# Two spectral layers and two feed-forward layers: row loads in quarters, shorter runs of zero products, statistics and residual sums placed elsewhere, the last inverse step's copies divided differently

## The chip, the cores and the metric

The kernel runs on one core of one Trainium2 chip. The metric is device time in microseconds (us) of one execution. Five executions of the kernel before the change were timed: 927.07, 926.19, 929.46, 926.41 and 926.54 us, so the median is 926.54 us. One of them (927.07 us) was recorded by the hardware profiler, and every duration below that is not a median comes from this record. Engines are written as the profile writes them: PE is TensorE, PEld its weight load, DVE is VectorE, ACT is ScalarE, POOL is GpSimd, SP is SyncE, which here only issues DMAs. A small q behind an engine's name means its sequencer.

## The reference

`x` has 2048 tokens (rows) of 1024 features in bf16. Four residual layers follow one another: A, B, A, B, the two A layers with the same weights and the two B layers with the same weights.

```python
def _A_ref(x, w_r, w_i):                      # 2D real FFT, a filter, and back
    X = rfft2(x) * (w_r + 1j * w_i)
    return irfft2(X, s=(2048, 1024))

def _B_ref(x, w1, b1, w2):                    # 1024 -> 3584 -> 1024
    h = x @ w1 + b1
    return (h * tanh(softplus(h))) @ w2       # the Mish activation

x = x + _A_ref(_layernorm(x)); x = x + _B_ref(_layernorm(x), ...)
x = x + _A_ref(_layernorm(x)); x = x + _B_ref(_layernorm(x), ...)
```

The layer norm takes mean and variance of every token over its 1024 features.

## The kernel before

**Program and waits.** The Python code writes out five instruction lists, one for each engine, in a fixed order. `op` and `group` record what an instruction reads and writes as resources (`Res`), and from them follow the semaphores that it waits for. An engine runs its list strictly in the order written, so an instruction that waits holds up everything behind it on its engine. A PSUM bank is a resource too: a copy out of a bank is noted as a writer of that bank, so a second copy from the same bank on another engine waits for the first.

**Residual stream.** `XS` holds x in SBUF as 16 tiles of 128 tokens. Statistics of a tile come either from DVE (`stats_half`, `stats_quarter`: bn_stats and bn_aggr, lines 466 to 486) or from ACT (`stats_act`, line 446): one pass with Copy and one with Square over 1024 features, each followed by a read of its accumulator. `sums_to_mv` and `scales` on DVE make mean and reciprocal root of these, and `apply` (line 522) makes the normalised tile.

**Start.** In layer 0 (the first A) SP first issues the loads of x into `XS`, then loads x a second time in another arrangement, `XR` (lines 399 to 407, issued at line 251): partition = (block of 128 tokens, feature block), 128 rows of 128 features each. This comes as one half and two quarters of the rows, each in 8 DMAs with 256-byte pieces. `r_xr` says which part a block of step s1 waits for. Behind them on SP follow the table FD, which step s2 reads, the table JT, the filters and more tables. Meanwhile DVE and ACT take the statistics of all 16 tiles.

**Layer A.** s1 (lines 619 to 647) multiplies the 16 blocks of 8 rows by the first transform matrices; in layer 0 each block has its own matrices, scaled by `scaled` with the norm (lines 604 to 617, on DVE, POOL and, for block 1, ACT). Copies out of PSUM (lines 640, 642) are on ACT and DVE. Then the list of `order_A` (line 1006) interleaves steps s2, s3, i1, i2 for 8 groups g: a word such as 310 means step 3, group 1, part 0; 4 is i1, 5 is i2. s3 ends with four DVE products (lines 800 to 807) whose result YK is what i1 (line 842) reads. PSUM is handed out as a ring of four pairs of banks in this order. i2's result goes out to HBM and comes back transposed (`u_turn`, `u_last`) as UT, in four parts for the last step i4 (line 1071).

**End of layer A.** While UT comes back, PE does `spin` (4 products), `residual_first` (8 products that put the old x into PSUM, line 1060) and `hold` (line 656): 16 products in layer 0 and 11 in layer 1 with a matrix of zeros, 128x512, which change nothing and only keep PE at work. Then, in `layer_B` from line 1507, i4 is done for tiles 0 to 3 in four parts u of 32 columns; `out_first` (line 1076) copies tiles t and t+1 of part u, 512 elements per partition, to `XS`, and `stats_quarter` takes the statistics of the part. After part 3, `root` and `apply` give the first two normalised tiles, PE transposes them (line 1181) and the first matrix product of layer B can start.

**Layer B.** `mm1` (line 1220) multiplies w1 by normalised tokens, into three PSUM banks in turn; ACT applies Mish (line 1224). `rest` mixes in the rest of i4 for tiles 4 to 15, whose result lies in `YS` until `residual` (line 1498, DVE) adds it to `XS`. The rest of w1's product is done in `quads` (lines 1250 to 1320) as a Strassen-like scheme of seven products for each of 14 blocks n (line 1260), with DVE additions (line 1265) and Mish on ACT (line 1270); `after(n)` puts statistics, `normal` and `residual` of later tiles between them. The product with w2 (line 1359) has the same kind of scheme.

Of the kernel before, what the change touches and what calls it, by code (L numbers as in the profile page):

```python
# [5 lines left out]
ACT = mybir.ActivationFunctionType  # L6
ALU = mybir.AluOpType
P = 128
# [172 lines left out]
class KB:  # L181
# [200 lines left out]
    def prologue(self):  # L382
        sp = self.sp
        self.op(self.pool, lambda e: e.memset(self.EPS[:], 1e-5), writes=[self.r_eps, self.r_warm])
        xt = self.x[0].rearrange("(t p) d -> p t d", p=P)

        for a, b in ((10, 11), (0, 1), (1, 2), (11, 12), (2, 3), (3, 4), (12, 13), (4, 6), (13, 14), (6, 8), (14, 15), (8, 10), (15, 16)):
            self.dma(self.act if a == 10 else sp, self.XS[:, a:b, :], xt[:, a:b, :], f"x{a}", writes=self.r_xs[a:b])
        self.warm(ACT.Sqrt)
        small = {}  # L390
        def load_small(name, n, d):
            b = self.alloc(name, self.o[name], [n], d)
            self.dma(sp, b.ap, self.con[name], name.lower(), writes=[b.res])
            small[name] = b
        load_small("M0", P, BF)
        load_small("IDF", P, F32)
        self.M0, self.IDF = small["M0"], small["IDF"]

        self.XR = self.alloc("XR", self.o["XR"], [P, P])
        self.r_xr = []  # L400
        xv = self.x[0].rearrange("(n2 n1) (h l) -> h n2 n1 l", n2=16, l=P)
        for q, n in ((0, 2), (2, 1), (3, 1)):
            r = Res(f"xr{q}")
            for h in range(8):
                s = slice(32 * q, 32 * (q + n))
                self.dma(sp, self.XR.ap[h:P:8, s, :], xv[h][:, s, :], f"xr{q}", parts=[r])
            self.r_xr += [r] * n
        self.dma(sp, self.FD[:], self.con["FD"], "fd", writes=[self.r_fd])
        load_small("JT", 4 * P, BF)
        self.JT, self.r_jt = small["JT"].ap, small["JT"].res  # L410
        self.w1_next = 0
# [31 lines left out]
                writes=rr)  # L443
        self.op(self.dve, lambda e: e.reciprocal(r, a), writes=rr)

    def stats_act(self, j):
        act = self.act
        x, sums, rs, junk = self.XS[:, j, :], self.BN[:, j, 0:2], self.r_mv[j], self.junk
        rs.begin()
        for i, f in enumerate((ACT.Copy, ACT.Square)):  # L450
            self.op(act, lambda e, i=i, f=f: e.activation(junk.ap, x, f, accum_out=sums[:, i:i + 1]),  # L451
                    reads=[self.r_xs[j]], writes=[junk.res], parts=[rs])

# [257 lines left out]
    def layer_A(self, li):  # L711
# [7 lines left out]
        dve, act, sp, pool = self.dve, self.act, self.sp, self.pool  # L719
# [275 lines left out]
                u_turn(g, h)  # L995
        self.spin(4, 0)
        self.residual_first()
        self.hold(11 if li else 16, 7)
        if li == 0:
            self.op(self.pool, lambda e: e.tensor_copy(self.B1[:], self.B1h[:]), reads=[self.r_b1h], writes=[self.r_b1])  # L1000
        self.w1_buf = [self.alloc(f"W1_{i}", (self.ob["WS"] + i * 4096, 140 * K)[i > 4], [8, 256]) for i in range(4 if li else 6)]
# [3 lines left out]
    @staticmethod  # L1005
    def order_A():


        order = ("200 201 210 211 300 301 220 310 400 221 311 401 230 320 410 500 231 321 411 501 330 331 420 510 240 511 421 241 "
                 "250 251 340 341 520 350 430 260 521 431 440 261 351 441 530 531 360 361 270 450 451 271 540 541 550 551 460 370 "  # L1010
                 "461 371 560 561 470 471 570 571")
        return [tuple(map(int, w)) for w in order.split()]
# [60 lines left out]
                                               stop=lo > 0 or l % k == k - 1))  # L1073
        self.group(fns, reads=self.r_ut[u0 // 32:(u0 + n - 1) // 32 + 1] + [self.r_mt], writes=self.r_bank[bank:bank - (-n // k)])

    def out_first(self, u, t, prog):

        b = slice(2 * u, 2 * u + 2)
        src = self.PS[:, b, :].rearrange("p b (i c) -> p c b i", c=32)[:, 8 * t:8 * t + 16]
        dst = self.XS[:, t:t + 2, :].rearrange("p n (h l) -> p (n h) l", l=P)[:, :, 32 * u:32 * u + 32]  # L1080

        self.copy(prog, dst.rearrange("p c (b i) -> p c b i", i=16), src, [], self.r_bank[b], parts=self.r_xs[t:t + 2])

    def i4_out(self, lo, nb, u0, n, bank, staged, r_staged, prog):

# [71 lines left out]
    def layer_B(self, li, last):  # L1157
        pe, dve, act, sp, pool = self.pe, self.dve, self.act, self.sp, self.pool
# [47 lines left out]
        def mm1(c, fg, half=None, mid=()):  # L1206
            wb = self.w1_buf[fg]
            x = XT[c]
            tok = slice(0, 512) if half is None else slice(256 * half, 256 * half + 256)
            w = tok.stop - tok.start  # L1210
            for fl in range(2):
                if fl:
                    for f in mid:
                        f()
                ft = 2 * fg + fl
                bank = nh[0] % 3
                nh[0] += 1
                fns = []
                for db in range(8):
                    fns.append(lambda e, db=db, bank=bank, fl=fl: e.matmul(  # L1220
                        PS[:, bank, 0:w], wb.ap[:, db, fl * P:(fl + 1) * P], x.ap[:, db, tok], start=(db == 0), stop=(db == 7)))
                self.group(fns, reads=[wb.res] + (r_xt[c] if half is None else [r_xt[c][half]]), writes=[self.r_bank[bank]])
                at, ra = at_of(c, ft), r_at[c % 2][ft]
                self.op(act, lambda e, bank=bank, ft=ft, at=at: e.activation(at[:, tok], PS[:, bank, 0:w], ACT.Mish,  # L1224
                                                                      bias=self.B1[:, ft:ft + 1]),
                        reads=[self.r_bank[bank], self.r_b1], writes=[ra])
# [246 lines left out]
        def at_tiles(c):  # L1473
            r_at[c] = [None] * NF
            for k in range(2):
                off = self.ob["A"] + 14336 * (2 * k + c)
                AT[c][k] = b = self.alloc(f"AT{c}{k}", off, [NF // 2, 512])
                for i in range(NF // 2):
                    r = r_at[c][2 * i + k] = Res(f"AT{c}_{2 * i + k}")
                    r.inherit(b.res)  # L1480
                    self.live.append((off + i * 1024, off + i * 1024 + 1024, r))
# [8 lines left out]
        def staged_rest(bank, n):  # L1490

            u0 = self.u0
            self.u0 += n
            self.i4(4, 12, u0, n, bank)
            return lambda: self.i4_out(4, 12, u0, n, bank, YS, r_ys, act)
# [5 lines left out]
        def turns(c, *ts):  # L1501
            return [lambda t=t: transposed(c, t, xn[4 * c + t]) for t in ts]
# [4 lines left out]
        for u in range(4):  # L1507
            self.i4(0, 4, 32 * u, 32, 2 * u)
            if u == 0:
                self.hold(2, 7)  # L1510
            self.out_first(u, 0, act)
            for j in range(2):
                self.stats_quarter(j, u)
            if u == 0:
                self.out_first(0, 2, dve)
        rests = [staged_rest(0, 10)]
        for u in range(1, 3):
            self.out_first(u, 2, act)
# [34 lines left out]
            xn[j] = self.apply(j)  # L1553
        for fg in range(1, 4):
            mm1(0, fg, 1)
            if fg < 3:
                self.stats_act(5 + fg)
        if not last:
            mm1(0, 4)
        at_tiles(1)  # L1560
        B = {"B11": (XT[0].ap[:, 0:4, :], r_xt[0]), "B21": (XT[0].ap[:, 4:8, :], r_xt[0])}
        order = list(early)
        if last:
            block, corner, run = quads(list(range(4, 14)), order, B, [k * 1024 for k in (102, 140)])
            for n, bank in ((0, 3), (1, 4), (2, 5), (3, 0)):
                block(n, bank)
            corner(1, 4)
            turns(1, 0)[0]()
            corner(2, 5)
            turns(1, 1)[0]()  # L1570
            corner(3, 0)
        else:
            mm1(0, 5, mid=turns(1, 0, 1))
# [50 lines left out]
        def after(n):  # L1624
            again = {0: 7, 4: 8, 5: 9} if last else {0: 7}
            if n in again:
                self.fill_slot(order[again[n]], plain + again[n])
            if 1 <= n < 4:
                load_b(STD, n // 3, (n - 1) % 2)
            first = 6 if last else 4  # L1630
            if last:
                if n in (0, 2, 4, 5):
                    self.stats_act(8 + (0, 2, 4, 5).index(n))
                if n == 5:
                    self.xn_buf = self.xn_out + [self.alloc(f"XN{i}", self.ob["XN2"] + i * 2048, [self.D]) for i in range(2)]
                if n in (5, 7):
                    self.sums_to_mv(n + 3, 2)
                    self.scales(n + 3, 2)
            elif n < 4:
                self.stats_dve(8 + n)  # L1640
            elif n == 4:
                self.scales(8, 4)
            if n >= first:
                normal(8 + n - first)
                turn(4)
            for j in {first + 1: (12, 13), first + 2: (14,), first + 3: (15,)}.get(n, ()):
                residual(j)
        run(after, lead)
        self.junk = self.alloc("JUNK2", self.ob["JUNK2"], [self.D])
# [68 lines left out]
        order = [ws[n % 3] for n in range(14)]  # L1718
# [94 lines left out]
```

## Time and profile before

| | |
|---|---|
| median of five executions | 926.54 us (926.19 to 929.46) |
| the profiled execution: its time, its span | 927.07 us, 925.2 us |
| busy in the span: PE, DVE, ACT, POOL | 876.8, 623.4, 434.9, 147.7 us |
| granted TensorE clock | 1.000 |
| layer 0 A; layer 0 B; layer 1 A; layer 1 B (from the timeline, rounded) | 0 to 111; 111 to 474; 474 to 560; 560 to 925 us |

The span runs from the first to the last recorded instruction; 1.87 us of the execution lie around it. A row of the timeline or of the chain has the start in us from the span's start, the duration in us, the engine and the line of the kernel; `x8` means that eight instructions were merged; what stands in brackets is the idle time of the engine before the row and what ended it. A row of the waits reads: engine and line, what ended its wait, us in total, times, the longest in us. The end of a matmul is modelled, so the start-to-start distance of two matmuls is a better measure than the shown idle time: 8 products of 128x256 follow one another every 0.87 us, 4 of 128x512 every 0.86 us.

### The profile page before, as it was taken

What the parts mean: (1) busy time and instruction counts of PE and PEld (TensorE: products, weight loads), DVE (VectorE), ACT (ScalarE), POOL (GpSimd) and SP (SyncE); (2) the same over time, 40 slices, a digit from 0 to 9 for tenths busy, and PEclk for the clock granted to TensorE, in tenths of its full rate; (3) what the DMA queues carried; (4) which work ended last, traced back from release to release, by engine and by line L of the source; (5) the groups of instructions that cost most, each with busy time, mean ns of one, the idle gap of its engine ahead of it and who ended that gap; (6) DMA issues with size and microseconds to landing.
All of it is one profiled execution on the core that took longest, in us unless ns stands there. A gap on an engine that the chain in (4) does not pass through costs nothing.

```text
span 925.2 us, 13610 instructions
## 1 busy us (share of the span) xinstructions
PE 876.8 (95%) x5503; PEld 470.2 (51%) x5503; DVE 623.4 (67%) x995; ACT 434.9 (47%) x645; POOL 147.7 (16%) x170
## 2 busy tenths in 40 slices
PE   0899899999999999999999998999999999999998
PEld 0677576444444444444446766754444444444443
DVE  7798468686889667568767765666747655554463
ACT  7898485456203475510018966757550025552000
POOL 0732004950004642010121200000000000000000
PEclk9999999999999999999999999999999999999999
DMA  9979962675796388274733786345156635732532
GB/s 279 279 254 289 224 186 72 213 256 133 265 287 232 143 322 293 107 248 140 269 92 115 224 213 161 137 167 183 32 196 187 207 139 182 274 120 85 176 125 103
DMA packets 153502, 175.98 MB, mean 190 GB/s; under 512 B 75000, under 2 KB 132568, under 8 KB 153320
## 3 DMA queue, kind: packets, MB, share of 16 engines
q1 hardware_dynamic: 140256, 130.32, 45.8%
q0 software_dynamic: 10032, 42.90, 12.6%
q10 hardware_dynamic: 3152, 1.90, 0.8%
q8 instruction: 43, 0.70, 0.3%
q14 instruction: 19, 0.16, 0.0%
HBM read 130.78 MB, written 40.89 MB: 186 GB/s over the span
## 4 chain that ended last, share of the span: by engine, by line
PE 86%; DVE 6%; ACT 4%; SPq 2%; DMA 2%; issue 1%; ACTq 0%; DVEq 0%
PE PS L1359 37%; PE PS L1260 30%; PE PS L1220 6%; PE PS L741 3%; PE PS L842 2%; SPq L251 2%; PE PS L872 2%; PE PS L1071 2%; ACT ARENA L640 1%; PE PS L1181 1%; ACT ARENA L451 1%; PE PS L904 1%; DVE ARENA L1186 1%; DMA ARENA<-in_A_x_dram 1%; ACT ARENA L573 1%
## 5 line engine op out<-in xcount | busy, mean ns | idle before, releaser
L1359 PE MATMUL PS<-ARENA 128*128 128x512 bf16 x1568 | 340.3, 379 | 0.1
L1260 PE MATMUL PS<-ARENA 128*128 128x512 bf16 (+1 forms) x1288 | 280.3, 379 | 0.8 <-DVE ARENA L1265 0.8
L1359 PEld LDWEIGHTS PS<-ARENA 128*128 128x128 bf16 x1568 | 153.2, 98 | 184.9 <-DVE ARENA L1402 0.5
L1265 DVE TENSOR_TENSOR ARENA<-PS,ARENA 128x512 f32<-128x512 f32 x230 | 157.0, 690 | 100.2 <-PE PS L1260 92.5
L1260 PEld LDWEIGHTS PS<-ARENA 128*128 128x128 bf16 x1288 | 125.4, 98 | 153.2 <-DVE ARENA L1265 3.5
L1270 ACT ACTIVATE ARENA<-ARENA,B 128x512 bf16<-128x512 f32 x138 | 98.8, 721 | 69.1 <-DVE ARENA L1265 63.8
L573 ACT ACTIVATE ARENA<-PS 128x512 f32<-128x512 f32 (+3 forms) x86 | 61.6, 726 | 110.6 <-PE PS L1260 92.5
L1153 POOL TENSOR_TENSOR ARENA<-ARENA 128x512 bf16<-128x512 bf16 x56 | 71.0, 1269 | 75.1 <-DVE ARENA L522 60.9
L451 ACT ACTIVATE ARENA<-XS 128x1024 bf16<-128x1024 bf16 x60 | 63.2, 1053 | 36.7 <-DVE XS L1410 33.2
L1220 PE MATMUL PS<-ARENA 128*128 128x256 bf16 (+1 forms) x528 | 73.4, 295 | 3.4 <-DVE ARENA L1186 1.9
L1384 DVE TENSOR_TENSOR ARENA<-ARENA 128x3584 bf16<-128x3584 bf16 x32 | 63.9, 2016 | 0.0
L1220 PEld LDWEIGHTS PS<-ARENA 128*128 128x128 bf16 x528 | 50.3, 98 | 22.3 <-DVE ARENA L1186 3.3
L1410 DVE TENSOR_TENSOR XS<-PS,ARENA 128x512 bf16<-128x512 f32 x52 | 35.7, 689 | 38.4 <-PE PS L1359 38.1
L1402 DVE TENSOR_TENSOR ARENA<-PS,ARENA 128x512 f32<-128x512 f32 x48 | 32.9, 687 | 27.4 <-PE PS L1359 27.0
L1224 ACT ACTIVATE ARENA<-PS,B 128x256 bf16<-128x256 f32 (+1 forms) x66 | 33.0, 514 | 29.0 <-PE PS L1220 28.8
L1270 ACT ACTIVATE ARENA<-PS,B 128x512 bf16<-128x512 f32 x46 | 31.5, 685 | 18.4 <-PE PS L1260 18.4
L1398 DVE TENSOR_TENSOR ARENA<-ARENA,XS 128x512 f32<-128x512 f32 x52 | 37.0, 735 | 0.6
L442 ACT ACTIVATE RS<-MV,EPS 128x1 f32<-128x1 f32 (+2 forms) x11 | 3.3, 296 | 71.5 <-DVE MV L564 70.1
L842 PE MATMUL PS<-ARENA 128*128 128x256 bf16 x256 | 32.6, 273 | 1.3 <-DVE ARENA L807 1.0
L741 PE MATMUL PS<-FD,ARENA 128*128 128x256 bf16 (+1 forms) x256 | 31.4, 271 | 2.5 <-ACT ARENA L640 2.5
L798 ACT ACTIVATE ARENA<-PS 128x1024 bf16<-128x1024 f32 x30 | 30.4, 1046 | 5.0 <-PE PS L789 5.0
L1235 DVE TENSOR_TENSOR ARENA<-ARENA 128x2048 f16<-128x2048 bf16 x16 | 25.3, 1582 | 9.0 <-PE PS L1220 8.7
(102 smaller groups left out, 810.1 us busy)
## 6 DMA issues: line engine op xcount, KB each, us to landing
ARENA<-in_B_w_dram SPq DMA_DIRECT2D x30, 896.0 KB, 6.6
ARENA<-w1s_scratch SPq DMA_DIRECT2D x28, 896.0 KB, 4.7
ARENA<-w2s_scratch SPq DMA_DIRECT2D x24, 896.0 KB, 6.3
w1s_scratch<-ARENA POOLq DMA_DIRECT2D x14, 896.0 KB, 4.3
ARENA<-in_B_w_dram SPq DMA_DIRECT2D x24, 512.0 KB, 4.5
u_scratch<-ARENA SPq DMA_DIRECT2D x14, 512.0 KB, 4.7
ARENA<-u_scratch SPq DMA_DIRECT2D x14, 512.0 KB, 5.9
w2s_scratch<-ARENA POOLq DMA_DIRECT2D x8, 896.0 KB, 4.1
```

The lines of the kernel that those rows point to most:

```text
L451: self.op(act, lambda e, i=i, f=f: e.activation(junk.ap, x, f, accum_out=sums[:, i:i + 1]), reads=[self.r_xs[j]], writes=[junk.res], parts ...
L573: fn = (lambda e: e.activation(dst, src, ACT.Copy)) if scale is None else \
L741: fns.append(lambda e: e.matmul(dst, at(r), FD[:, t:t + n], start=start, stop=stop))
L842: fns.append(lambda e, c=c, part=part: e.matmul(ps[:, c * 256:(c + 1) * 256], yk.ap[:, part, c * P:(c + 1) * P], t[:, (128, 0)[part]:(384, ...
L1153: self.op(self.pool, lambda e, dst=A(dst), x=A(x), y=A(y), op=op: e.tensor_tensor(dst, x, y, op), reads=[b.res] + list(after), writes=[b.rs])
L1220: fns.append(lambda e, db=db, bank=bank, fl=fl: e.matmul(PS[:, bank, 0:w], wb.ap[:, db, fl * P:(fl + 1) * P], x.ap[:, db, tok], start=(db ...
L1260: self.group([lambda e, db=db: e.matmul(PS[:, bank, :], A[:, db, :], mov[:, db, :], start=(start and db == 0), stop=(db == 3), skip_group_ ...
L1265: self.op(dve, lambda e: e.tensor_tensor(dst.ap, PS[:, bank, :], x.ap, ALU.add), reads=[self.r_bank[bank], x.res], writes=[dst.res])
L1270: self.op(act, lambda e: e.activation(at, src, ACT.Mish, bias=self.B1[:, ft:ft + 1]), reads=[res, self.r_b1], writes=[ra])
L1359: self.group([lambda e, i=i, k=k, b=PB[n][k].ap: e.matmul(PS[:, bank, :], ap[:, i, t * P:(t + 1) * P], b[:, i - 7 * k, :], start=(start an ...
L1384: self.op(dve, lambda e: e.tensor_tensor(ap[dst][:, f, :], ap[x][:, f, :], ap[y][:, f, :], op), reads=part(x, k) + part(y, k), writes=part ...
L1398: self.op(dve, lambda e: e.tensor_tensor(a[t], a[t], x, ALU.add), reads=[rx], writes=[r[t]])
```

## The change

Six places change.

1. `XR` is loaded in four quarters of the rows, 8 DMAs and a resource of its own each: 32 DMAs in place of 24, of the same bytes in the same 256-byte pieces.
2. `hold` does 12 zero products in place of 16 in layer 0, and 5 in place of 11 in layer 1.
3. In `order_A`, 221 (s2 of group 2, part 1) stands ahead of 400 (i1 of group 0, part 0) and no longer behind it. This holds for both A layers.
4. `out_first` takes a number of tiles. In part 3, ACT copies tile 0 and DVE tile 1 (256 elements each) where ACT copied both; in part 0, tiles 2 and 3 are copied by ACT and no longer by DVE. This holds for both B layers.
5. `stats_act` can do one of its two passes. The four passes for tiles 6 and 7 stood in pairs behind two of the `mm1` calls; now one pass stands behind each of three, and the fourth behind `mm1(0, 4)` (layer 0) or behind the first `corner` (layer 1).
6. In the last layer, `residual` of tiles 12 and 13 stands at n = 1 and n = 3 of `quads`, where both stood at n = 7. Tiles 14 and 15 stay at n = 8 and 9, and the first B layer keeps its places.

```diff
-        for q, n in ((0, 2), (2, 1), (3, 1)):
+        for q in range(4):
             r = Res(f"xr{q}")
             for h in range(8):
-                s = slice(32 * q, 32 * (q + n))
+                s = slice(32 * q, 32 * q + 32)
                 self.dma(sp, self.XR.ap[h:P:8, s, :], xv[h][:, s, :], f"xr{q}", parts=[r])
-            self.r_xr += [r] * n
+            self.r_xr.append(r)
...
-    def stats_act(self, j):
+    def stats_act(self, j, passes=(0, 1)):
...
-        rs.begin()
-        for i, f in enumerate((ACT.Copy, ACT.Square)):
+        if passes[0] == 0:
+            rs.begin()
+        for i in passes:
+            f = (ACT.Copy, ACT.Square)[i]
...
-        self.hold(11 if li else 16, 7)
+        self.hold(5 if li else 12, 7)
...
-        order = ("200 201 210 211 300 301 220 310 400 221 311 401 ...
+        order = ("200 201 210 211 300 301 220 310 221 400 311 401 ...
...
-    def out_first(self, u, t, prog):
+    def out_first(self, u, t, prog, n=2):
...
-            self.out_first(u, 0, act)
+            if u < 3:
+                self.out_first(u, 0, act)
+            else:
+                self.out_first(u, 0, act, 1)
+                self.out_first(u, 1, dve, 1)
             for j in range(2):
                 self.stats_quarter(j, u)
             if u == 0:
-                self.out_first(0, 2, dve)
+                self.out_first(0, 2, act)
...
         for fg in range(1, 4):
             mm1(0, fg, 1)
-            if fg < 3:
-                self.stats_act(5 + fg)
+            self.stats_act(6 + fg // 3, ((fg - 1) % 2,))
         if not last:
             mm1(0, 4)
+            self.stats_act(7, (1,))
...
             corner(1, 4)
+            self.stats_act(7, (1,))
             turns(1, 0)[0]()
...
-            for j in {first + 1: (12, 13), first + 2: (14,), first + 3: (15,)}.get(n, ()):
+            late = {1: (12,), 3: (13,), 8: (14,), 9: (15,)} if last else {5: (12, 13), 6: (14,), 7: (15,)}
+            for j in late.get(n, ()):
                 residual(j)
```

## The prediction

> **What bounds the kernel now.** I read the page first, then the waits of PE stage by stage, then the chain in order of time, then the timeline around each edit.
>
> ```profile
> span 925.2 us, 13610 instructions
> ...
> PE 876.8 (95%) x5503; PEld 470.2 (51%) x5503; DVE 623.4 (67%) x995; ACT 434.9 (47%) x645; POOL 147.7 (16%) x170
> ...
> PE 86%; DVE 6%; ACT 4%; SPq 2%; DMA 2%; issue 1%; ACTq 0%; DVEq 0%
> ```
>
> PE is busy for 95% and carries 86% of the chain, and no edit but the zero products takes work from it. So the change is worth what it takes out of PE's waits. The waits of PE in three windows (116 to 474, 482 to 566, 566 to the end) show which of them the edits touch:
>
> ```profile
> PE PS L1220 <- ACT ARENA L1224: 0.8, 2, 0.6
> ```
> ```profile
> PE PS L1071 <- DMA ARENA<-u_scratch: 0.9, 1, 0.9
> ...
> PE PS L842 <- DVE ARENA L807: 0.6, 1, 0.6
> ```
> ```profile
> PE PS L1260 <- DVE ARENA L1265: 0.8, 1, 0.8
> PE PS L1220 <- ACT ARENA L1224: 0.6, 1, 0.6
> ```
>
> The other PE waits in the two B layers (0.9, 0.9 and 0.4 us) belong to the transposes, and none is for a DMA. What is gained at these places should therefore arrive at the end: behind them the DMAs are released by PE's own progress and move with it.
>
> **Rows in quarters.** In the timeline SP's queue reads, in two windows (last part of the half, then quarters):
>
> ```profile
> 14.25 6.04 SPq L251 DMA_DIRECT2D ARENA<-in_A_x_dram  x5
> ```
> ```profile
> 20.34 11.27 SPq L251 DMA_DIRECT2D ARENA<-in_A_x_dram  x16
> ```
>
> A half costs 6.04/5 = 1.21 us of SP, a quarter 0.63 us and 0.67 us apart (the first, 1.20 us, still queues behind the halves). Before 14.25 the queue is held up by the loads of x, and three of the 8 half DMAs are out. In quarters that is 6, and 26 x 0.67 = 17.4 us more end at 31.7; FD is issued at 31.65 now. So nothing behind the rows (FD, JT, filters, tables, all on SP) moves by more than some 0.3 us. The first quarter lands near 19 us in place of 24.33, so s1 no longer waits 3.2 us for it, but for its matrices: DVE's first product ends at 22.73, and ACT is in block 1's matrices until 24.08. ACT's first copy goes from 25.45 to 24.1. This lead is lost by the end of s1: block 12 needs the last quarter, landed at 33.81, and starts at 33.85 now; s2 starts at 38.01, FD has landed at 37.65, and the first filter, read right after s2's first group (39.54), at 39.34. I take 0, from 0.1 less to 0.5 more.
>
> **Zero products.** The chain in order of time, layer 0 and layer 1:
>
> ```profile
> 107.36 3.45 PE PS L656 x16
> 110.82 0.79 PE PS L1071 x32
> ...
> 555.22 4.87 DMA ARENA<-u_scratch
> 560.23 0.95 PE PS L1071 x32
> ```
>
> In layer 0, UT's first part lands at 110.22, and i4 begins at 110.65 because 16 x 0.216 us of zeros end only then. Twelve end at 109.75. In layer 1 i4 starts 0.14 us after the landing (560.09), so here 110.36: 0.29 less, and part 1 (landed 111.16, needed at 111.6) doesn't take it back. In layer 1 PE waits for the landing either way: six zeros less lengthen its idle time from 1.1 to 2.4 us and gain nothing, 0. What this idle time costs is not in the trace: after 1.3 us idle (at 491.93) PE goes on at full pace; after 3.2 us (24.38) the first 8 products of s1 took 1.05 us, later ones 0.62. At the worst ratio, 1.7, on the 3.8 us of i4 and its two zeros, that is 2.5 us. I take 0, as the same 32 products took 0.95 us after 1.1 us idle and 0.95 after none; 2.5 stays as the upper end.
>
> [...]
>
> **The order of s2 and i1.** In layer 1 PE finishes s3(1,0) at 498.66 and waits for the DVE product until 499.47 (0.80 us start to start), while the s2 that stands behind i1 has its inputs. With s2(2,1) first, PE runs 498.67 to 499.54, i1 follows at once (YK is there at 499.41), and s3(1,1) starts 0.82 us earlier. ACT, busy back to back from 500.55 on, starts at 499.9 with s2's copy. DVE's products are back to back until 505.53 and stay there, but its next gap (0.66 us at 506.19, waiting for ACT) closes. The next i1 has to wait for its YK (501.41). Neither step issues a DMA. I take 0.65 less, from 0.8 to 0. In layer 0 the same swap gains nothing: DVE and ACT run without a gap from 43 to 57 us there, and PE waits for DVE at 58.36 in any case.
>
> **Copies.** Window 114.6 to 117 of the timeline, part 3 of i4 in layer 0:
>
> ```profile
> 114.31 1.23 DVE L482 BATCH_NORM_STATS2 BN<-XS 128x6 f32<-128x256 bf16 x3
> ...
> 114.48 1.57 ACT L573 ACTIVATE XS<-PS 128x512 bf16<-128x512 f32 x3 [0.20 <-PE PS L1071]
> ...
> 115.57 0.26 DVE L484 BATCH_NORM_AGGREGATE MV<-BN 128x2 f32<-128x24 f32 x1
> ```
>
> Everything after this hangs on DVE: two statistics, two aggregates, root, apply, then PE (117.58). ACT's copy of both tiles ends at 115.08, and DVE, which ends part 2's statistics at about 115.0, starts the next at 115.11. So ACT was hardly late. Now ACT's half copy ends at 114.88 (0.60 less 256 elements at 0.85 ns), DVE's copy waits for it as the bank's earlier writer, stands ahead of the statistics in DVE's queue and takes 0.41 us (0.67 for 512 elements, less 256 at 1.07 ns; overlapped with the next, 0.34). The statistics start at 115.35: 0.24 later, in both layers, 0.5 more (0.2 to 0.9). Part 0's copy on ACT fits its gap (112.24 to 112.88), and takes 0.67 us from DVE where DVE waits for ACT anyway: 0.
>
> [...]
>
> **Statistics of tiles 6 and 7.** The chain says what PE waited for at 139.27 and 142.21:
>
> ```profile
> 137.70 1.15 ACT ARENA L451 x2
> 139.58 1.05 ACT ARENA L451 x2
> 140.65 1.15 ACT ARENA L451 x2
> 142.21 3.63 PE PS L1220 x16
> ```
>
> Four passes of 1.17 us come in pairs between Mish operations, and PE, with three banks, needs the Mish of three products ago. Its product due at 138.49 (137.62 + 0.87) started at 139.27: 0.78 lost; the one due at 141.89 started at 142.21: 0.32. In layer 1 one such loss, 588.84 in place of 588.06: 0.78. With one pass for each pair of Mish (0.83 us): first pass 136.52 to 137.68, Mish of the third product 137.70 to 138.16, ahead of 138.49; the later Mish end at 138.5, 140.1, 140.5 and are needed at 139.4, 141.1, 142.8. ACT does 2.0 us for PE's 1.74 in this stretch, so it falls back 0.26 a step, for three steps, and the banks carry that. Square of tile 7 ends at 144.75 (595.2 in layer 1); DVE asks for it at 146.4 (595.8) after the transposes' copies. So 1.10 + 0.78 = 1.9 less; if ACT's load only shifts the wait, 0.8.
>
> **Residual sums.** The chain again, last layer:
>
> ```profile
> 659.63 1.20 DVE XS L1498 x2
> 660.83 0.61 DVE ARENA L1265
> 661.49 4.49 PE PS L1260 x20
> ```
>
> Two residuals stand in DVE's queue ahead of the addition that frees PE's bank. PE's product was due at 660.76 and started at 661.49: 0.73. Without them the addition starts at 659.6. At n = 1 and n = 3 DVE is idle for 1.03 and 1.63 us, against 0.65 us of a residual, so they are hidden there; without that cover each would cost at most its 0.65. I take 0.7 less (0.4 to 0.9).
>
> **The sum.** 0 - 0.3 + 0 - 0.65 + 0.5 - 1.9 - 0.7 = -3.05 us. The profiled execution would take 927.07 - 3.05 = 924.0 us. It lies 0.53 above the median, so the median goes from 926.54 to 923.5 us.
>
> **Rivals.** (1) ACT, not the order of its passes, is the bound between 134 and 145 us: the PE waits move to a later product, 1.1 us of the 1.9 stay, and the median is 924.6 or, with the order's gain lost too, 925.3. For it: ACT has no gap from 134.3 to 143.1. Against it: its work ends 1.05 us before the Mish at 144.15. (2) The longer idle time in layer 1 slows PE: 2.5 us, 926.0. It decides once 2.4 us are enough; 3.2 us after a long rest is the nearest row. (3) Slower: a quarter costs SP as much as a half. At 1.21 us, 16 issues take 19.4 us where the 8 halves took 12.8 (7.54 to 20.34), FD and the filters land 6.6 us later and s2 starts with them: 923.5 + 6.6 = 930.1. The point of balance is 3.05 us, that is 12.8 + 3.05 = 15.9 us for 16, 0.99 us each. Against it: 15 quarters in a row at 0.67. (4) The spreading doesn't spread: the copies cost 0.9 in place of 0.5 and the passes give 0.8 in place of 1.9, so 1.5 less is gained, 925.0. DVE's and ACT's back-to-back rows speak for it, the free banks worked out above against it.
>
> **How the numbers follow.** Chances: forecast 0.74, (1) 0.10, (2) 0.06, (3) 0.04, (4) 0.06. The range of the forecast's own terms reaches from 922.8 (order 0.8, copies 0.2, residuals 0.9) to 924.7 (rows 0.5, copies 0.9, order 0.3); taking in (1) and (4) makes it 922.7 to 925.4. A measurement here can tell 0.2%, 1.85 us, from no change: faster is under 924.69. The forecast's case lies there nearly whole, and half of (1): 0.77. Within 0.2%: the rest of (1), (2), (4) and a little of the forecast, 0.19. Slower: (3), 0.04.
>
> **What would show it.** The waits of PE should have lost L1220 <- ACT L1224 in both B layers and L1260 <- DVE L1265 in the last; L842 <- DVE L807 in layer 1 should shrink to about 0.1; the wait for u_scratch should grow to 2.2 us, with the 32 products behind it still at 0.95. Between part 3's last product and the first transpose 3.1 us should become 3.3. s2 should start within 0.3 us of 38.0. I am wrong if FD lands after 38.5, if ACT's passes still stand in PE's way, or if i4 of layer 1 slows.

## The result, and the profile after

The kernel after the change takes 931.86 us (median of 27 executions, 927.32 to 937.13). The kernel before, executed beside it and in later sets of runs, takes 928.69 us (median of 48; the five shown above were 926.54). The ratio is 1.0031, 95% interval 1.0020 to 1.0043: about 3 us slower, where 3 us faster was predicted.

The profiled execution of the kernel after took 928.3 us, 1.2 us more than the one of before; it is one of the shorter executions of this kernel, and shows only part of the loss. Lines of the kernel behind `stats_act` are two higher than before (L1220 became L1222). The page:

```profile
span 926.4 us, 13601 instructions
...
PE 877.5 (95%) x5493; PEld 473.1 (51%) x5493; DVE 623.3 (67%) x995; ACT 435.5 (47%) x647; POOL 148.7 (16%) x170
...
PE 87%; DVE 5%; SPq 4%; DMA 3%; ACT 2%; issue 1%; ACTq 0%; DVEq 0%
```

PE has ten instructions fewer, and yet is busy 0.7 us longer: some of them took longer. The waits of PE, in four windows (24 to 116, 116 to 474, 482 to 566 us, and from 566 us on, where none is left that an edit was to remove):

```profile
PE PS L636 <- DVE ARENA L617: 2.6, 1, 2.6
```
```profile
PE PS L1183 <- DVE ARENA L524: 1.2, 1, 1.2
```
```profile
PE PS L636 <- DMA ARENA<-ARENA: 3.7, 1, 3.7
PE PS L1073 <- DMA ARENA<-u_scratch: 1.6, 1, 1.6
```

The three waits that the change was to take away are gone in all windows: L1222 for ACT's Mish (both B layers), L1262 for DVE's addition, L844 for DVE's product in layer 1. The chain in order of time shows PE at work without a break where the statistics and where the residual sums stood in its way:

```profile
135.98 10.31 PE PS L1222 x71
```
```profile
655.90 11.22 PE PS L1262 x52
```

New is a wait of 2.6 us in s1 of layer 0. The name after the arrow is that of the release seen last, a DVE product that ended at 35.01 for block 15; block 12's own matrices were ready at 30.70, and what it waited for is the fourth quarter, landed at 35.00. At the wait of 3.7 us at the start of layer 1 no edit stands: a store of xn issued at 471.83 landed at 477.36 (before: 471.65 and 474.49), and such stores take from 2.8 to 5.5 us within one trace. It comes up again at the end of the experiments. What follows these waits is the main thing. PE in s1 by the timeline, first block 12 before the change, then two rows after it, then the table of busy time over successive stretches of the same execution; its columns are the stretch, its length, then busy time (instructions) of PE, PEld, DVE, ACT and POOL, the granted clock of PE, DMA share and GB/s:

```profile
33.95 1.76 PE L634 MATMUL PS<-ARENA 128*128 128x128 bf16 x24 [0.39 <-DVE ARENA L642]
```
```profile
31.78 0.62 PE L636 MATMUL PS<-ARENA 128*128 128x128 bf16 x8 [0.30 <-ACT ARENA L642]
35.05 3.52 PE L636 MATMUL PS<-ARENA 128*128 128x128 bf16 x32 [2.64 <-DVE ARENA L617]
```
```profile
31.76:35.17 3.41, 0.74 (x11) 0.58 (x12) 3.25 (x3) 1.80 (x2) 1.03 (x2) 1.00 0.93 186
35.17:38.58 3.41, 3.39 (x32) 3.12 (x30) 0.83 (x1) 1.94 (x2) 0.00 (x0) 0.50 0.95 285
```
```profile
482.30:485.70 3.40, 0.94 (x17) 0.97 (x18) 0.29 (x1) 0.00 (x0) 0.00 (x0) 1.00 0.02 5
485.70:489.10 3.40, 3.40 (x37) 3.40 (x34) 2.88 (x3) 2.05 (x2) 0.00 (x0) 0.50 0.00 0
```

After a stretch of 3.41 us in which PE was busy for 0.74 or 0.94 us, the granted clock is 0.50 for exactly the next such stretch. In it eight products of s1 follow one another in 0.85 us in place of 0.45. The quietest stretches of the kernel before, in the same kind of table, keep the full clock:

```profile
35.10:38.50 3.40, 1.73 (x21) 1.36 (x22) 2.20 (x2) 2.48 (x3) 1.34 (x2) 1.00 0.95 257
```
```profile
564.20:567.60 3.40, 1.78 (x34) 1.45 (x31) 2.84 (x9) 3.00 (x7) 0.00 (x0) 1.00 1.03 298
```

The clock column needs one caution. The clock record of each of the 14 profiles begins at 27.0 to 30.2 us only (before 28.32, after 28.34); ahead of that the products of s1 follow one another every 107 ns, the pace of the stretch at 0.50 above, behind it every 56 ns, the pace at 1.00. So s1 starts at the half-clock pace before and after the change, though the column reads 1.00 there. The 1.05 us of the first eight products, which the prediction weighed as the price of 3.2 us of idle time, is this.

The mean granted clock of all timed executions says the same as the tables: 0.9928 for the kernel after, 0.9980 for the kernel before in the first set of experiments. A stretch of 3.41 us at half clock lowers the mean of an execution by 0.0018 (half of 3.41 us, of 930 us), so these are 2.8 more of them in each execution. Each costs at most 1.71 us of PE's work, half its length, together 4.8 us: an estimate from these two figures.

The executions of the kernel after, compared with one another, agree: the six with a clock of 0.996 or more took 927.3 to 929.4 us, the five with 0.990 or less 933.0 to 937.1. A straight line through all 28 rises by 1.6 us for every 0.0018 of clock and would stand at 925.0 us at full clock; lines through the executions of before in the three sets would stand at 927.2 to 927.8. That is an extrapolation, as no execution of after had the full clock, and the line can't part a stretch at half clock from a longer wait ahead of it.

### The profile page after: what moved, and what is told of

It is laid out like the page before. It is cut to its first block, busy times and chain, and to the rows that moved or that the text cites. A ratio compares the mean times of both kernels' runs of the same rounds, so it can differ in the third digit from the quotient of the medians.

```text
span 926.4 us, 13601 instructions
## 1 busy us (share of the span) xinstructions
PE 877.5 (95%) x5493; PEld 473.1 (51%) x5493; DVE 623.3 (67%) x995; ACT 435.5 (47%) x647; POOL 148.7 (16%) x170
## 4 chain that ended last, share of the span: by engine, by line
PE 87%; DVE 5%; SPq 4%; DMA 3%; ACT 2%; issue 1%; ACTq 0%; DVEq 0%
PE PS L1361 36%; PE PS L1262 30%; PE PS L1222 7%; SPq L251 4%; PE PS L743 2%; PE PS L844 2%; PE PS L874 2%; PE PS L1073 2%; PE PS L1183 1%; DMA ARENA<-in_A_w_i_dram 1%; ACT ARENA L642 1%; PE PS L906 1%; DMA xn_scratch<-ARENA 1%; PE PS L788 1%; DVE ARENA L1188 1%
## 5 line engine op out<-in xcount | busy, mean ns | idle before, releaser
L1262 PE MATMUL PS<-ARENA 128*128 128x512 bf16 (+1 forms) x1288 | 280.2, 379 | 0.0
L1262 PEld LDWEIGHTS PS<-ARENA 128*128 128x128 bf16 x1288 | 125.5, 98 | 152.1 <-DVE ARENA L1267 2.1
L1222 PE MATMUL PS<-ARENA 128*128 128x256 bf16 (+1 forms) x528 | 72.9, 295 | 2.0 <-DVE ARENA L1188 1.9
L1412 DVE TENSOR_TENSOR XS<-PS,ARENA 128x512 bf16<-128x512 f32 x52 | 35.6, 689 | 38.6 <-PE PS L1361 38.3
L1222 PEld LDWEIGHTS PS<-ARENA 128*128 128x128 bf16 x528 | 50.5, 98 | 20.1 <-DVE ARENA L1188 3.3
L844 PE MATMUL PS<-ARENA 128*128 128x256 bf16 x256 | 32.6, 273 | 0.3 <-DVE ARENA L831 0.2
```

The source lines that it names most:

```text
L844: fns.append(lambda e, c=c, part=part: e.matmul(ps[:, c * 256:(c + 1) * 256], yk.ap[:, part, c * P:(c + 1) * P], t[:, (128, 0)[part]:(384, ...
L1222: fns.append(lambda e, db=db, bank=bank, fl=fl: e.matmul(PS[:, bank, 0:w], wb.ap[:, db, fl * P:(fl + 1) * P], x.ap[:, db, tok], start=(db ...
L1262: self.group([lambda e, db=db: e.matmul(PS[:, bank, :], A[:, db, :], mov[:, db, :], start=(start and db == 0), stop=(db == 3), skip_group_ ...
```

## The experiments

**Theories.** A: the rows in quarters leave PE idle in s1, and the clock is halved behind that. B: the shorter runs of zero products do the same ahead of i4. C: the copies, or something else among the other edits, do it or eat the gain in another way. Against all three stands what was predicted: that no edit costs more than 0.5 us. All kernels were timed in five rounds beside the kernel before. "Clock" is the mean granted clock over a kernel's executions, and the last column that of the kernel before in the same set of runs.

| kernel | median us | ratio to before, 95% interval | clock | before's clock |
|---|---|---|---|---|
| a_rows_back | 930.62 | 1.0024 (1.0009 to 1.0038) | 0.9942 | 0.9980 |
| a_holds_back | 929.03 | 1.0005 (0.9986 to 1.0024) | 0.9931 | 0.9980 |
| a_both_back | 927.46 | 0.9998 (0.9978 to 1.0019) | 0.9947 | 0.9980 |
| b_holds | 931.07 | 1.0019 (1.0004 to 1.0034) | 0.9970 | 0.9980 |
| a_s1_fill | 928.48 | 1.0002 (0.9987 to 1.0017) | 0.9973 | 0.9986 |
| b_osr | 923.74 | 0.9957 (0.9941 to 0.9974) | 0.9990 | 0.9986 |
| b_copies | 931.05 | 1.0035 (1.0018 to 1.0052) | 0.9961 | 0.9986 |
| a_both_fill | 925.63 | 0.9978 (0.9967 to 0.9989) | 0.9995 | 0.9986 |
| after2 | 932.35 | 1.0039 (1.0023 to 1.0055) | 0.9912 | 0.9982 |
| a_fill | 927.68 | 0.9990 (0.9980 to 1.0000) | 0.9998 | 0.9982 |
| best | 925.99 | 0.9966 (0.9952 to 0.9979) | 0.9999 | 0.9982 |
| b_rows | 929.60 | 1.0005 (0.9994 to 1.0016) | 0.9960 | 0.9982 |

**First set: rows and zero products undone.** From the kernel after, the rows' loads are put back (a_rows_back), the zero products (a_holds_back), or both (a_both_back); b_holds is the kernel before with the shorter runs alone.

```diff
# a_rows_back, a_both_back
-        for q in range(4):
+        for q, n in ((0, 2), (2, 1), (3, 1)):
# a_holds_back, a_both_back (b_holds: the reverse, on the kernel before)
-        self.hold(5 if li else 12, 7)
+        self.hold(11 if li else 16, 7)
```

> The changed kernel with only the row loads as before (one half and two quarters). Theory A (rows): the quarters are limited by SP's issue, the last one lands 1.2 us later, PE idles 2.6 us in s1 and its clock is halved for one window, so with them undone s2 starts again at 38.0 and the time falls by 2 to 3 us against the changed kernel: ratio to before about 1.000. Theory B (holds): the rows are a small part and the lost time comes from half-clock windows behind the shortened zero products: ratio stays at 1.002 or more and the granted clock below 0.995. Theory C (copies): neither matters, 1.003.

> The changed kernel with only the zero products as before (16 and 11). Theory A: within 0.5 us of the changed kernel, ratio 1.003. Theory B: the mean granted clock rises by 0.002 or more and the time falls by 2 to 4 us, ratio 1.000 or below. Theory C: 1.003.

> The changed kernel with rows and zero products both as before; order, copies, statistics and residual sums stay changed. Theories A and B together: the four remaining edits give their -0.8 + 0.5 - 1.9 - 0.8 = -3.0 us, ratio 0.997. Theory C (copies or something else eats the gain): 1.000 or above.

> The kernel before with only the shortened zero products (12 and 5). Theory A: within 0.3 us of before, ratio 1.000, clock as before. Theory B: 1.002 to 1.004, with a lower granted clock and half-clock windows near 111 or 560 us in some executions. Theory C: 1.000.

Each undone edit brings time back (0.7, 2.6 and 3.3 in a thousand, against the kernel after), but with both undone the kernel only equals the one before, though four edits with a forecast of 2.75 us are still in it, and its clock stays low, 0.9947. This points to a part for A, a part for B and a third part, theory C. The shorter zero products alone make the kernel before 1.9 in a thousand slower. Their forecast gain is in the profile all the same: i4 of layer 0 starts 0.4 us earlier against the spin ahead of it in b_holds than before (7.36 against 7.76 us). The intervals overlap, so how much is due to each of the two edits is not to be had from these four runs. Nor is it all clock where the zero products are concerned: with them undone the time falls by 2.4 us, but the clock, 0.9931, is hardly above after's 0.9928, where theory B had expected 0.002 more; and b_holds is 1.8 us slower than before with a clock only 0.0010 lower, worth 1 us at most.

**Second set: the rest of the edits, and PE kept busy.** b_copies and b_osr are the kernel before with the copies alone, and with order, statistics and residual sums alone. The other two fill PE's idle time with products whose sums are never read, a_s1_fill in s1 of the kernel after, and a_both_fill in a_both_back ahead of the first transposes.

```diff
# a_s1_fill, ahead of block 12 of s1 in layer 0
+            if not li and j == 12:
+                self.group([lambda e: e.matmul(self.PS[:, 6, :], XR.ap[:, 0, :], XR.ap[:, 0:4, :], start=True, stop=True)] * 10,
+                           reads=[self.r_xr[0]], writes=[self.r_bank[6]])
# a_both_fill, besides the two edits undone
+        self.hold(4, 7)
         for j in range(2):
             transposed(0, j, xn[j])
```

> The kernel after with ten products of 128x512 of rows that are already there, ahead of s1's block 12 in layer 0 (their sums are never read); rows stay in quarters. They take 2.15 us of PE's 2.64 us idle time while it waits for the fourth quarter. If this idle time is what halves the clock behind it (theory A), the rows' blocks 12 to 15 start at 35.05 us as after, run at 0.45 us a block again, s2 starts near 38.3 us in place of 39.7, no half-clock window stands at 35 us, and the time falls by 1.2 to 1.7 us against after's 931.9. If the late last quarter alone is the loss (rival), the clock there stays halved or s2 still starts at 39.7, and the time stays within 0.5 us of 931.9 or is longer.

> The kernel before with the order, the statistics and the residual sums of the change and without its rows, zero products and copies. By the profiled shifts these three are worth 0.8 + 1.9 + 1.0 = 3.7 us, and none of them touches PE's idle stretches ahead of i4 or in s1. If the half-clock windows come from rows, zero products and copies (theories A, B and C), the mean clock is that of before (0.998) and the time 3.2 to 3.8 us under before, a ratio of 0.9960 to 0.9966. If any shift of work brings half-clock windows (rival), the mean clock falls to 0.995 and the ratio is 0.998 to 1.001.

> The kernel before with the copies of the change alone: part 3 divided over ACT and DVE, tiles 2 and 3 of part 0 on ACT. By the profile the first transposes come 0.4 us later in layer 0 and 0.2 us later in layer 1, so 0.6 us more, a ratio of 1.0007, if nothing else happens. If PE's longer wait ahead of the transposes also brings half-clock windows (theory C), the mean clock falls below 0.997 and the time is 1.5 to 2.5 us over before.

> The kernel after with rows and zero products as before (16 and 11), and four zero products of 128x512 more in both B layers, between the last product of i4's part and the first transposes, where PE waits for DVE. They take 0.86 us of 1.3 to 1.5 us. If half-clock windows behind i4 are what keeps the kernel with both parts undone at a ratio of 0.9998 (theory C), the mean clock rises from 0.9947 towards 0.998 and the time falls by 1 to 2 us, a ratio of 0.997 to 0.9985. If the windows are decided elsewhere, the ratio stays at 0.9995 to 1.001.

a_s1_fill decides on theory A. Nothing is taken from the change, ten products are added, and the kernel is 3 in a thousand faster than after; its clock rises from 0.9928 to 0.9973. The table of stretches, over the same two as in the kernel after:

```profile
31.76:35.17 3.41, 2.73 (x17) 1.34 (x18) 3.26 (x3) 1.81 (x2) 1.30 (x2) 1.00 0.61 134
35.17:38.58 3.41, 1.82 (x30) 1.68 (x31) 0.58 (x1) 1.48 (x2) 0.00 (x0) 1.00 0.86 262
```

PE is busy for 2.73 us in place of 0.74, and the next stretch has the full clock. But one expectation failed: s2 starts at 40.06 us, not near 38.3. The fourth quarter came later still in this execution (landed at 36.40, after at 35.00), so here the loads cost time at full clock too.

b_copies is the largest single loss, 3.5 in a thousand with an interval from 1.8, where the copies' own delay is 0.2 us a layer in its profile (i4 to the first transpose: 7.11 us in both layers against 6.93 and 6.92 before). The rest goes with the clock, 0.9961 (table of stretches, around the first transposes of layer 1):

```profile
567.77:571.18 3.41, 1.61 (x32) 1.28 (x29) 2.94 (x10) 2.62 (x6) 0.00 (x0) 1.00 1.20 307
571.18:574.59 3.41, 2.62 (x22) 2.05 (x20) 2.74 (x5) 3.38 (x5) 0.00 (x0) 0.50 0.75 191
```

Not all of this is theory C's place. The same profile has a half-clock stretch in s1 and s2 of layer 0, where the copies change nothing, behind one that stood at 1.73 us in the kernel before:

```profile
35.27:38.68 3.41, 1.44 (x23) 1.15 (x21) 2.10 (x2) 2.75 (x3) 1.44 (x2) 1.00 0.91 229
38.68:42.09 3.41, 3.39 (x19) 2.30 (x18) 0.43 (x1) 1.42 (x2) 3.06 (x5) 0.50 1.02 353
```

With four zero products at the transposes, a_both_fill has no half-clock stretch before the end, its clock is 0.9995, and it is 2 in a thousand faster than a_both_back, though the intervals overlap. In its profile the zero products put the first transposes off by 0.58 us in each layer (7.69 us from i4 to them, a_both_back 7.11): in layer 0 they waited 1.20 us themselves, for a copy of ACT out of the bank that they write to. By the medians they are worth more than that.

b_osr shows the other side: three edits that remove waits of PE and lengthen none keep the clock (0.9990) and give 4.3 in a thousand, 4.0 us, as forecast or a little more.

**Third set: the whole account.** after2 is the kernel after, unchanged, on the chip of this set. a_fill has every edit but the shorter zero products, with both fills. b_rows is the kernel before with the quarters alone. best is b_osr with 13 zero products in layer 0 and the four ahead of the transposes:

```diff
# best, besides order, statistics and residual sums
-        self.hold(11 if li else 16, 7)
+        self.hold(11 if li else 13, 7)
+        self.hold(4, 7)
         for j in range(2):
             transposed(0, j, xn[j])
```

> The kernel after, unchanged, beside the others of this call. If after's lower clock belongs to the kernel and not to the chip that it ran on (theories A, B and C), its mean clock is 0.992 to 0.994 here too, and the ratio 1.002 to 1.0045. If it was the chip (rival), the clock is that of before and the ratio 0.997 to 0.998.

> The kernel after with every edit but the zero products (16 and 11 as before), and with work in PE's idle time: the ten products in s1 and the four zero products ahead of the first transposes. If low activity of PE in three places is the whole of what the change loses (theories A, B and C together), the mean clock rises to 0.998 or more and what the five other edits give is seen: 924 to 926 us, a ratio of 0.996 to 0.998. If the rows or the copies lose time by themselves (rival), the clock rises but the ratio stays over 0.999.

> The kernel before with order, statistics and residual sums of the change, 13 zero products in place of 16 in layer 0 (the first product of i4 followed the 16th without a gap, and 12 gave 0.66 us), 11 in layer 1, and four zero products ahead of the first transposes. If the windows follow PE's activity, the clock stays at 0.999 and the time is 0.3 to 0.9 us under that of order, statistics and residuals alone: a ratio of 0.9945 to 0.9955. If three products fewer in layer 0 bring a half-clock window (rival), the ratio is 0.996 to 0.998.

> The kernel before with the rows in quarters alone. If the idle time ahead of the fourth quarter halves the clock behind it (theory A), the mean clock falls to 0.995 to 0.997 and the time is 1.3 to 2.5 us over before, a ratio of 1.0014 to 1.0027, with a half-clock window at about 35 us. If the quarters cost nothing by themselves (what was predicted), the ratio is 0.9995 to 1.0005.

after2 rules the chip out: 0.9912 beside a kernel before at 0.9982. a_fill rises to 0.9998 with every edit but the shorter zero products still in it, and PE's low activity is thereby shown to be what lowers this kernel's clock; but at 0.9990 it misses its expected 0.996 to 0.998. Two things were left out of that expectation: the four zero products cost 0.58 us in each of two layers, as above, and the quarters' own delay (s2 starts at 39.55, before at 38.01, both at full clock). The rival named there, that rows or copies lose time by themselves, fits the rows.

best misses its range too: 0.9966 in place of 0.9945 to 0.9955, for the same 1.15 us of zero products, which it didn't need, as b_osr's clock had been 0.9990 without them. Its interval and b_osr's overlap. Both beat the kernel before and after; b_osr, the simpler, is the version to keep.

b_rows has half-clock stretches one behind the other. Its mean clock is as expected (0.9960), its ratio less than expected (1.0005). In its profile the clock stays at half for three stretches:

```profile
30.98:34.39 3.41, 1.21 (x19) 0.86 (x16) 2.79 (x3) 2.59 (x3) 1.89 (x2) 1.00 0.86 194
34.39:37.80 3.41, 2.51 (x24) 2.52 (x25) 0.70 (x1) 1.44 (x2) 0.00 (x0) 0.50 0.92 256
37.80:41.20 3.40, 2.24 (x17) 1.69 (x15) 1.23 (x1) 1.52 (x2) 2.01 (x3) 0.50 1.00 267
41.20:44.60 3.40, 3.40 (x20) 2.50 (x19) 1.37 (x2) 2.40 (x4) 2.70 (x4) 0.50 1.08 404
```

2.51 and 2.24 us busy at half clock are 1.26 and 1.12 us when counted half, and the next stretch is halved again; 3.40 us are 1.70, and the profile shows the full clock after it. Why three such stretches cost the whole kernel so little here isn't settled: PE also waits for DMAs in these places (the tables and filters behind s2), and the runs don't say how much of the lost time those waits would have taken anyway.

**Where the half-clock stretches lie.** In the 14 profiles they stand in four places, not in three. In s1 and s2 of layer 0: in four of the six kernels with quarters (the other two have the ten products there), and in b_copies. At i4 of layer 1: in two of the five kernels with the shorter runs of zero products (a_rows_back, b_holds). At the first transposes of layer 1: in four of the seven kernels with the copies and without zero products there. The fourth place is the start of layer 1 (after, after2, a_rows_back, b_holds): PE had waited there for 3.1 to 3.8 us, in the ten other profiles for 2.1 us at most. These four are all among the five kernels with the shorter runs. The longer wait costs time beside the clock and fits what a_holds_back and b_holds show; but how a shorter run of zero products, over 360 us earlier, would bring it about, or whether it is chance, these runs don't say.

## Why the prediction was wrong, step by step

**Statistics, residual sums, order: right.** Between the shifts of PE's instructions against before, the statistics of layer 0 took 1.13 us (forecast 1.10), of layer 1 0.79 (0.78), the residual sums 0.96 (0.7), the order in layer 1 0.81 (0.65). The sum is 3.7 us against 3.25, and b_osr gave 4.0 us in the median (interval 2.4 to 5.5). The rival that spreading doesn't spread, and the one that ACT is the bound, are out: no wait for ACT's Mish is left.

**Zero products: not steady. Copies: near their size.** i4 of layer 0 gained 0.66 us between spin and i4 in the profile of after and 0.40 in that of b_holds (forecast 0.3). In the three other profiles with 12 zero products (a_rows_back, a_s1_fill, after2) spin and i4 lie 7.85 to 8.04 us apart, before 7.76: there PE waited for UT's landing, and nothing was gained. The copies cost 0.40 us in layer 0 and 0.19 in layer 1 (forecast 0.24 each; 0.18 and 0.19 in b_copies). The chain shows the copies in the order that was forecast: DVE's half behind ACT's, and the statistics behind both.

```profile
115.95 0.39 ACT XS L575
...
116.36 0.42 DVE XS L579
116.79 0.34 DVE BN L484
```

**Rows: mis-sized.** Forecast was 0, with FD and the filters in their old places. The step that failed is the count of what SP has out before the queue of the loads lets go at about 14 us: six quarters were assumed (as many bytes as three halves), and it was four. The 28 others follow 0.67 us apart, as forecast:

```profile
16.04 16.74 SPq L251 DMA_DIRECT2D ARENA<-in_A_x_dram  x25
32.83 0.62 SPq L251 DMA_DIRECT2D FD<-c_fd  x1
```

So FD is issued at 32.83 in place of 31.65 and lands at 38.09, ahead of the 38.5 that was to be a sign of error; but the last quarter lands at 35.00 in place of 33.81. As s2 starts 1.2 us after the last block of s1, whose block 12 waits for this quarter, s2 starts at 39.55 even at full clock (a_fill), 1.5 us later than before. Over all profiles s2 starts at 39.55 to 41.47 with quarters and at 37.94 to 39.30 without. As in rival (3), SP's issue is the limit, though a quarter cost 0.67 us as forecast, and the delay is a quarter of that rival's. How much of it reaches the end is less sure: the whole loss of b_rows, delay and clock together, is 0.5 us, and by its interval at most 1.5.

**The clock: the step that turned the sign.** The step of the prediction that failed is the 0 that it put for PE's idle time. With the terms as measured the sum would still be a gain: 3.7 + 0.66 - 0.59 - 1.5 = 2.3 us, an estimate from single profiles. Measured are 2.9 us more (0.0031 of 928.7), so 5.2 us are left, and 2.8 more half-clock stretches make up to 4.8 of them. That PE's low activity is behind a large part is shown by a_s1_fill: ten added products in one gap bring the ratio from 1.0031 to 1.0002. What the shorter zero products lose beside the clock stays open. The prediction had this mechanism in one place only, as rival (2): a longer idle time in layer 1 ahead of i4, at 2.5 us and a chance of 0.06, deciding "once 2.4 us are enough". It took the question to be how long one gap is. The other two places weren't looked at: the lead of PE in s1 was noted ("this lead is lost by the end of s1"), but not that an earlier start against a last quarter that comes no earlier gathers the idle time in one gap, 0.39 us ahead of block 12 before and 2.64 after; and the longer way to the first transposes was only a delay of 0.24 us.

The traces show stretches of a fixed length, and no empty ones. In the kernel after the granted clock was 0.50 for 3.413 us twice, from 35.17 and from 485.73 us, and these starts lie 132 times 3.413 us apart. In all profiles every full-clock stretch that cost the next one its clock had PE at work, for 0.62 to 1.69 us of its 3.41. The prediction put 0 for 2.4 us of idle time by the nearest rows of the trace of before, which show no loss after 1.1 and 1.3 us; how busy PE was in the whole stretch around such a gap it didn't ask.

**What the rest of the forecast got wrong by this.** The forecast gave slower a chance of 0.04, all of it to SP's issue cost. The quietest stretches of the kernel before were there to be seen, with PE busy for 1.73 and 1.78 us; that this lies right at the edge could not be read from that trace alone, since no stretch behind 28.32 us was halved in it. What half clock costs could be: 107 ns a product in place of 56 at the start of s1.

## What to carry to other kernels

Before waits are moved or zero products cut, list the kernel's quietest stretches of 3.4 us by PE's busy time. Here, by the count in the section below, all 16 with less than 1.40 us of 3.41 and six of 13 with 1.43 to 1.69 were followed by a stretch at half clock; where an edit takes one so low, count a possible 1.7 us for it (an estimate, half of 3.41) in each execution, as the place of the stretches differs from one execution to the next: the record's first begins at 28.34 us in after and at 28.71 in after2, the same kernel. An edit that lets PE start earlier against an unchanged end (a later DMA, a chain on another engine) gathers its idle time into one gap, here 2.64 us in place of 0.39, and can cost more than it gives; zero products or other work in such gaps held the clock (0.9973 in a_s1_fill against 0.9928, 0.9995 in a_both_fill against 0.9947), but they delay what follows where they have to wait themselves, as in a_both_fill for a PSUM bank, 1.20 us. The rows in smaller DMAs landed their first part earlier, at 19.12 in place of 24.33 us, and their last part later, at 35.00 in place of 33.81, with the queue that issues them as the limit: four quarters were out before it let go at 14.0 us, where as many bytes as in three halves would have been six. So count issues, not bytes.

## What the runs showed of the hardware

- **PE's busy time and the clock behind it.** In the record of after the clock changes at 35.17, 38.58, 485.73, 489.14 and 926.05 us, which are 1, 131, 1 and 128 times 3.413 us apart. So the records of all 14 profiles were cut into windows of 3.413 us, from where each begins to 12 us before the end: 3627 windows, with PE's busy time in each, counted half where the window itself was at half clock (107 ns a product of s1 there, 56 at full clock). Of 16 windows under 1.40 us all were followed by a window at half clock. Of 13 between 1.43 and 1.69 us, six were. Of the 3598 from 1.70 us on, none was. The busy time is the profile's, whose ends of matmuls are modelled, so the edge near 1.4 to 1.7 us belongs to this measure and to these products.
- **Half-clock windows in a row.** In the same count, seven of the 16 were at half clock themselves: PE was busy for 1.90 to 2.63 us of them, and the next was halved again, in b_rows and after2 for 10.2 us in a row. Behind half-clock windows with 3.10 us or more the full clock came back.
- **The kernel before.** Two of the quietest windows of the profiled kernel before stood at 1.74 and 1.80 us, and its executions ran at 0.9980 to 0.9986 on average, so some of them lost a window too.
